# Two weight chunks of the next expert split ahead of a branch, and the work around the join put in another order

## The chip, the core and the metric

The kernel runs on one core of a Trainium2 chip. The metric is the time of one execution on the device in microseconds (us), the median of the runs shown. The engines are TensorE (PE in the rows, its weight loads PEld), VectorE (DVE), ScalarE (ACT), GpSimd (POOL) and SyncE (SP), which issues most DMAs.

## The reference

Causal attention is followed by two mixture-of-experts layers on 1792 tokens of width 768. Each layer has 8 experts with two weight matrices (768 x 1024 and 1024 x 768); each token goes to one expert, and in the first layer about half of the tokens skip.

```python
for e in range(E):                       # first layer
    mask = e_idx == e
    h = np.maximum(xc[mask] @ w1[e], 0.0)
    y[mask] = gate_w[mask, None] * (h @ w2[e])
out[do_compute] = xc + y
...
for e in range(E):                       # second layer
    mask = expert_idx == e
    h = np.maximum(x[mask] @ w1[e], 0.0)
    out[mask] = gate_w[mask, None] * (h @ w2[e])
```

## The kernel before

Attention takes the first 235 us or so and is not touched. After it the sixteen experts (`i` = 0 to 15; `m` = 0 for the first layer, `i // 8`) run one after the other. The tokens of an expert are fetched by an index list (an indirect DMA on GpSimd, `gather`) in tiles of 128.

**Split operands.** All products are made of float32r parts: a weight chunk `raw` is split into an upper part `hi` (a cast on ACT, L734) and a lower part `lo` (raw minus hi on DVE, L738, written over `raw`). `w1` has six chunks of 128x1024 (`KC`), `w2` eight of 128x768 (`FC`). The tokens are transposed on PE (L752) in two halves, and each half is split in the same way into `xt`: the upper part on ACT (L758), the lower on DVE (L759). A first product (`layer1`, L779) of one half `u` of the hidden columns takes twelve matmuls on upper weight parts (token upper and token lower, for each of six chunks) and six on lower weight parts. Then the hidden tile goes through PE transposes (`turn_h`) and is split again (`split_ht`: ACT L770, DVE L771), and `layer2` (L787) takes six matmuls for each of the eight chunks `f`.

**A tile.** `Tile.begin` holds the first product, the splits of this expert's `w2` (`w2_high`, `w2_low`; in the first tile of an expert, and not for the first expert of a layer) and `layer2` for f = 0 to 5. `Tile.finish` holds `layer2` for f = 6 and 7, the transposes and splits of the next tile's tokens, the write of the result (`put_y`), and, in the last tile of an expert, the splits of all six `w1` chunks of the next expert and the DMA issues for a later one. Six rooms `hi1` hold the upper parts. In the second layer `begin` also computes the gate in steps (`gate_parts`, small DVE operations); in the first layer it routes the tokens of the tile before into the second layer (`route_enter`, `route_turn`, `route_logits`, `route_pick`, `route_rank`, and `route_put` in `finish`).

**The branch and the join.** How many tiles an expert has is known only on the chip. Behind the first `begin` stands `tc.If(nmore[e] > 0)` (L1096): with one tile all engines go straight to the last `finish`, with more they go through the further tiles first (a nested `If` at L1077). What stands behind the point where the paths join counts on semaphores whose values both paths must reach. On the path that skips, each engine adds the missing count itself when it has done all it has to do before the branch. So an instruction behind the join that needs another engine's earlier work waits until that engine has come to the join. A wait that the rows put down to `PEq L1096` or `DVEq L1077` is of this kind.

**Order.** The schedule is written out by hand: each engine takes its instructions in the order of the code. Experts 0, 1, 2, 3, 5, 6 of the first layer and 0, 4, 7 of the second (`i` = 8, 12, 15) have one tile in this data; `i` = 4, 9 and 13 have two, `i` = 10 three, `i` = 7, 11 and 14 four.

Of the kernel before, what the change touches and what calls it, by code (L numbers as in the profile page):

```python
# [8 lines left out]
F32R = mybir.dt.float32r  # L9
# [36 lines left out]
def moe_attention_kernel(tc, qk, vv, w_r, emb, tau, w11, w12, w21, w22, out):  # L46
# [25 lines left out]
    with ExitStack() as top:  # L72
# [612 lines left out]
        with ExitStack() as ctx:  # L685
# [4 lines left out]
            def keep(shape, dt, name, pool=wp):  # L690
                return pool.tile(shape, dt, tag=name, name=name)
# [3 lines left out]
            hi2 = [keep([P, DM], F32R, f"hi2_{j}") for j in range(FC)]  # L695
            xt = keep([P, KC, P, 2], F32R, "xt")
# [24 lines left out]
            def w1(i, k):  # L721
                n = KC * i + k
                return hi1[k], lo1[n % N1], raw1[n % N1]
# [49 lines left out]
            def layer1(i, u, ks, low):  # L773

                for k in ks:
                    wh, wl, _ = w1(i, k)
                    terms = [(0, wl)] if low else [(0, wh), (1, wh)]
                    for j, r in terms:
                        nc.tensor.matmul(p1[u], xt[:, k, :, j], r[:, u * 512 : (u + 1) * 512],  # L779
                                         start=(k == 0 and j == 0 and not low), stop=(k == KC - 1 and low))  # L780
# [159 lines left out]
            class Tile:  # L940
# [22 lines left out]

                def begin(self):
# [5 lines left out]
                    self.w2_low(0)  # L970
                    layer1(i, 0, range(KC), False)
# [3 lines left out]
                    layer1(i, 0, range(KC), True)  # L975
                    self.step()
                    self.w2_low(1)
# [5 lines left out]
                    layer1(i, 1, range(KC), False)  # L983
# [19 lines left out]
                    self.w2_low(5, 6)  # L1003
# [3 lines left out]
                    self.w2_low(7)  # L1007
                    split_ht(turned, 4)
                    layer2(i, 2)
                    layer2(i, 3)  # L1010
                    if route:
                        route_rank()
                    layer2(i, 4)
                    layer2(i, 5)

                def finish(self, idx, last, nxt, route):
# [14 lines left out]
                    high(0, 1, 2)  # L1031
# [5 lines left out]
                    low(0, 1, 2)  # L1037
# [3 lines left out]
                    high(3)  # L1041
                    low(3)
                    layer2(i, 6)
                    if route:
                        route_put()
                    if nxt is not None:
                        t = xt_turn(nxt, *HALVES[1])
                        xt_split(t, *HALVES[1])
                    layer2(i, 7)
# [3 lines left out]
                    high(4, 5)  # L1053
                    put_y(self.m, self.g, idx)
                    low(4, 5)
# [140 lines left out]
```

## Time and profile before

| | |
|---|---|
| median of 3 runs | 910.62 us (909.84 to 916.43) |
| the profiled execution | 913.13 us, its span 911.3 us |
| PE busy | 832.6 us, 91% of the span |
| DVE busy | 554.6 us, 61% |
| ACT busy | 474.3 us, 52% |
| mean granted TensorE clock | 0.979 of full speed |

The profiled execution takes 1.8 us more than its span, and 2.5 us more than the median. A busy PE is one with a matmul in flight; matmuls overlap, so an idle time that the profile shows is less than what a wait costs. The experts take from about 245 us to 902 us.

### The profile page before, as it was taken

How to read it: one execution, taken by the hardware profiler on the slowest of the kernel's cores; microseconds unless marked ns; L12 is line 12 of the kernel's file. 1: busy time of each engine (PE TensorE's matmuls, PEld its weight loads, DVE VectorE, ACT ScalarE, POOL GpSimd, SP SyncE). 2: the span in 40 equal slices, each digit the busy share in tenths (PEclk: the TensorE clock that was granted, in tenths of full speed). 3: DMA queues.
4: the chain of work that ended last, by engine and by line, in shares of the span. 5: the costliest groups of instructions: out<-in, count | busy, mean ns of one | idle time of the engine just before them, and what ended most of it. 6: DMA issues, size and time to landing. Idle time of an engine off the chain costs nothing. (4 is left out here: it accounts for less than half of the span.)

```text
span 911.3 us, 14892 instructions
## 1 busy us (share of the span) xinstructions
PE 832.6 (91%) x4960; PEld 682.8 (75%) x4960; DVE 554.6 (61%) x1641; ACT 474.3 (52%) x1013; POOL 163.3 (18%) x150
## 2 busy tenths in 40 slices
PE   8998989989788888998899979899999998899995
PEld 5666666666477776886699857788889887798884
DVE  5767767776567587387743265755383368483363
ACT  5777666766456366166631153654272267372362
POOL 1132404013211333032011011111020012021000
PEclk9999999999899899999999989999999999999998
DMA  7979555564646477167610172762171076371000
GB/s 219 326 266 302 165 183 163 166 218 125 197 168 243 158 294 284 63 237 294 262 65 27 67 269 67 286 257 110 56 296 37 37 306 228 126 271 51 19 29 7
DMA packets 59033, 158.23 MB, mean 174 GB/s; under 512 B 13013, under 2 KB 23765, under 8 KB 58448
## 3 DMA queue, kind: packets, MB, share of 16 engines
q1 hardware_dynamic: 52816, 139.33, 42.8%
q0 software_dynamic: 6080, 17.29, 5.3%
q8 instruction: 59, 0.97, 0.4%
q14 instruction: 78, 0.64, 0.2%
HBM read 146.45 MB, written 22.92 MB: 186 GB/s over the span
## 5 line engine op out<-in xcount | busy, mean ns | idle before, releaser
L738 DVE TENSOR_TENSOR lo<-raw,hi 128x768 fp32r<-128x768 f32 (+1 forms) x218 | 221.7, 1064 | 37.3 <-ACT hi L734 34.4
L787 PE MATMUL p<-hi,ht 128*128 128x384 f32 x960 | 240.8, 352 | 3.4 <-DVE ht L771 2.7
L779 PE MATMUL p<-hi,xt 128*128 128x512 f32 x720 | 184.8, 401 | 25.3 <-DVE xt L759 15.8
L734 ACT CAST hi<-raw 128x768 fp32r<-128x768 f32 (+1 forms) x218 | 187.3, 924 | 35.3 <-PEq L1096 29.9
L779 PEld LDWEIGHTS p<-hi,xt 128*128 128x128 f32 x720 | 138.1, 195 | 61.1 <-DVE xt L759 22.4
L787 PEld LDWEIGHTS p<-hi,ht 128*128 128x128 f32 x960 | 166.7, 190 | 11.5 <-DVE ht L771 7.3
L321 ACT ACTIVATE pr<-st,mn 112x336 f32<-112x336 f32 x192 | 99.5, 519 | 61.6 <-DVE mn L318 61.5
L787 PE MATMUL p<-lo,ht 128*128 128x384 f32 x480 | 123.6, 339 | 0.0
L771 DVE SCALAR_TENSOR_TENSOR ht<-tp,ht 128x512 fp32r<-128x512 f32 x60 | 41.4, 689 | 126.9 <-ACT ht L770 115.1
L779 PE MATMUL p<-lo,xt 128*128 128x512 f32 x360 | 100.8, 410 | 4.9 <-DVE lo L738 4.9
L787 PEld LDWEIGHTS p<-lo,ht 128*128 128x128 f32 x480 | 88.1, 189 | 0.0
L779 PEld LDWEIGHTS p<-lo,xt 128*128 128x128 f32 x360 | 67.1, 195 | 20.7 <-DVE lo L738 11.0
L938 ACT COPY hs<-p 128x512 f32<-128x512 f32 x60 | 34.9, 582 | 91.6 <-PE p L779 88.4
L318 DVE CUSTOM_DVE_ANT_0 st<-s,mask 112x336 f32<-112x336 f32 x144 | 63.5, 465 | 30.5 <-PE s L307 18.9
L770 ACT ACTIVATE ht<-tp 128x512 fp32r<-128x512 f32 x60 | 36.0, 600 | 77.4 <-PE tp L796 74.5
L758 ACT CAST xt<-tp 128x384 fp32r<-128x384 f32 (+2 forms) x62 | 30.3, 494 | 80.9 <-PE tp L752 74.2
L759 DVE TENSOR_TENSOR xt<-tp,xt 128x384 fp32r<-128x384 f32 (+2 forms) x62 | 33.5, 542 | 57.2 <-ACT xt L758 56.9
L741 POOL DMA_INDIRECT g_r<-x,L x14 | 32.3, 2308 | 166.0 <-DVE pv L813 97.0
L331 PE MATMUL tp<-ident,pr 112*112 112x112 f32 x480 | 58.0, 269 | 0.0
L816 POOL DMA_INDIRECT out<-py,pidx x18 | 23.7, 1318 | 187.7 <-DVEq L1077 70.8
L307 PE MATMUL s<-qk 64*112 64x112 f32 (+2 forms) x288 | 50.4, 456 | 6.3 <-DVE mn L318 6.2
L331 PEld LDWEIGHTS tp<-ident,pr 112*112 112x112 f32 x480 | 47.8, 138 | 8.9 <-issue 8.1
(201 smaller groups left out, 955.0 us busy)
## 6 DMA issues: line engine op xcount, KB each, us to landing
raw<-in_w SPq DMA_DIRECT2D x96, 512.0 KB
raw<-in_w SPq DMA_DIRECT2D x128, 384.0 KB
qk<-in_qk SPq DMA_DIRECT2D x23, 896.0 KB
x<-x SPq DMA_DIRECT2D x24, 448.0 KB
v<-in_vv SPq DMA_DIRECT2D x4, 1344.0 KB
qk<-in_qk SPq DMA_DIRECT2D x2, 448.0 KB
g_n<-x,L POOLq DMA_INDIRECT x23, 6.1
out<-py,pidx POOLq DMA_INDIRECT x18, 3.4
```

What stands on the lines that cost most here:

```text
L307: nc.tensor.matmul(a[c], src[r : r + 64, c * CP : (c + 1) * CP], src[r : r + 64, S : S + n], start=True, stop=True)
L318: nc.vector.tensor_tensor_reduce(out=so, in0=a[c], in1=mask[:, S - n : S], scale=-0.125, scalar=3.0e38, op0=ALU.add, op1=ALU.min, accum_ou ...
L321: return lambda: nc.scalar.activation(a["pr"][:, OFF[c] * CP : OFF[c] * CP + n], so, AF.Exp, bias=mn, scale=-1.0, accum_out=rs)
L331: nc.tensor.transpose(tp[:, u * CP : (u + 1) * CP], pr[:, o : o + CP], ident[:CP, :CP])
L734: copy(hi, raw)
L738: eng.tensor_tensor(lo, raw, hi.bitcast(F32), op=ALU.subtract)
L759: nc.vector.tensor_tensor(xt[:, a:b, :, 1], src, hi.bitcast(F32), op=ALU.subtract)
L770: nc.scalar.activation(hi, src, AF.Relu)
L771: nc.vector.scalar_tensor_tensor(lo, src, 0.0, hi.bitcast(F32), op0=ALU.max, op1=ALU.subtract)
L779: nc.tensor.matmul(p1[u], xt[:, k, :, j], r[:, u * 512 : (u + 1) * 512], start=(k == 0 and j == 0 and not low), stop=(k == KC - 1 and low))
L787: mm = nc.tensor.matmul(p2[u], l, r[:, u * (DM // 2) : (u + 1) * (DM // 2)], start=(f == 0 and j == 0), stop=(f == FC - 1 and j == len(ter ...
L938: nc.scalar.copy(hs[:, u * 512 : (u + 1) * 512], p1[u])
```

## The change

The number of rooms for upper parts of `w1` grows from six to eight, used in turn over all chunks of all experts. The first tile of an expert splits chunks 0 and 1 of the next expert (`ahead`) behind its `layer2(3)`, before the branch. In `finish` the DMA issues stand first, then the first half of the next tokens, and only then the splits of chunks 2 to 5; `route_put` and `put_y` stand last. In `begin` the first product takes four chunks of upper parts of half 0, three of half 1, then the rest of half 0 and the lower parts; `route_enter` and `w2_low(0)` move behind that, and `w2_low(6)` and `w2_low(7)` move behind the second `split_ht`.

```diff
+            hi1 = hi1 + [keep([P, DF], F32R, f"hi1_{j}") for j in range(KC, KC + 2)]
...
-                return hi1[k], lo1[n % N1], raw1[n % N1]
+                return hi1[n % len(hi1)], lo1[n % N1], raw1[n % N1]
...
+                def ahead(self, k):
+
+                    if self.first and self.i + 1 < len(experts):
+                        split_high(self.i + 1, k)
+                        split_low(self.i + 1, k, nc.vector)
+
                 def begin(self):
...
                     self.w2_high(0, 1, 2, 3)
-                    self.w2_low(0)
-                    layer1(i, 0, range(KC), False)
+                    layer1(i, 0, range(4), False)
+                    layer1(i, 1, range(3), False)
+                    layer1(i, 0, range(4, KC), False)
+                    self.step()
+                    layer1(i, 0, range(KC), True)
                     if route:

                         route_enter()
-                    layer1(i, 0, range(KC), True)
-                    self.step()
-                    self.w2_low(1)
+                    self.w2_low(0, 1)
                     copy_h(0)
...
-                    layer1(i, 1, range(KC), False)
+                    layer1(i, 1, range(3, KC), False)
...
-                    self.w2_low(5, 6)
+                    self.w2_low(5)
                     layer2(i, 0)
                     layer2(i, 1)
                     turned = turn_h(1)
-                    self.w2_low(7)
                     split_ht(turned, 4)
+                    self.w2_low(6, 7)
                     layer2(i, 2)
                     layer2(i, 3)
                     if route:
                         route_rank()
+                    self.ahead(0)
+                    self.ahead(1)
...
-                    high(0, 1, 2)
                     if last:
                         for k in range(KC):
                             load1(KC * i + k + N1)
                         for f in range(FC - 2):
                             load2(FC * i + f + N2)
-                    low(0, 1, 2)
                     if nxt is not None:
                         t = xt_turn(nxt, *HALVES[0])
                         xt_split(t, *HALVES[0])
-                    high(3)
-                    low(3)
+                    high(2)
                     layer2(i, 6)
-                    if route:
-                        route_put()
                     if nxt is not None:
                         t = xt_turn(nxt, *HALVES[1])
                         xt_split(t, *HALVES[1])
+                    low(2)
+                    high(3)
+                    low(3)
                     layer2(i, 7)
...
                     high(4, 5)
+                    low(4, 5)
+                    if route:
+                        route_put()
                     put_y(self.m, self.g, idx)
-                    low(4, 5)
```

On DVE, behind the join from expert 3 to expert 4, this stood before (`lo1` and `hi1` are parts of `w1` chunks with their room's number, `L864` to `L178` is `route_put`, `L804` is `put_y`):

```order
L738 TENSOR_TENSOR lo1_10_79<-raw1_10_65,hi1_0_115 128x1024
L738 TENSOR_TENSOR lo1_11_80<-raw1_11_66,hi1_1_116 128x1024
L738 TENSOR_TENSOR lo1_12_81<-raw1_12_67,hi1_2_117 128x1024
L759 TENSOR_TENSOR xt_3111<-tp_2_3129,xt_3111 128x384
L738 TENSOR_TENSOR lo1_13_82<-raw1_13_68,hi1_3_118 128x1024
L864 TENSOR_TENSOR run_165<-run_165,oh2_3141 128x8
```

And now, in the same place of DVE:

```order
L761 TENSOR_TENSOR xt_3113<-tp_2_3131,xt_3113 128x384
L761 TENSOR_TENSOR xt_3113<-tp_0_3129,xt_3113 128x384
L740 TENSOR_TENSOR lo1_12_81<-raw1_12_67,hi1_2_117 128x1024
L740 TENSOR_TENSOR lo1_13_82<-raw1_13_68,hi1_3_118 128x1024
L740 TENSOR_TENSOR lo1_0_69<-raw1_0_55,hi1_4_119 128x1024
L740 TENSOR_TENSOR lo1_1_70<-raw1_1_56,hi1_5_120 128x1024
L866 TENSOR_TENSOR run_165<-run_165,oh2_3143 128x8
```

Three lower parts of weights that stood ahead of the first half of the tokens are gone from there; the tokens are first, and four lower parts follow both halves.

On DVE, at the end of expert 4's first `begin`, up to the branch, this stood before (`ht` is the second `split_ht`):

```order
L738 TENSOR_TENSOR lo2_5_104<-raw2_5_88,hi2_5_3108 128x768
L738 TENSOR_TENSOR lo2_6_105<-raw2_6_89,hi2_6_3109 128x768
L738 TENSOR_TENSOR lo2_7_106<-raw2_7_90,hi2_7_3110 128x768
L771 SCALAR_TENSOR_TENSOR ht_3117<-tp_1_3128,ht_3117 128x4x128
L1096 COMPARE_AND_BRANCH
```

And now:

```order
L740 TENSOR_TENSOR lo2_5_104<-raw2_5_88,hi2_5_3108 128x768
L773 SCALAR_TENSOR_TENSOR ht_3119<-tp_1_3130,ht_3119 128x4x128
L740 TENSOR_TENSOR lo2_6_105<-raw2_6_89,hi2_6_3109 128x768
L740 TENSOR_TENSOR lo2_7_106<-raw2_7_90,hi2_7_3110 128x768
L740 TENSOR_TENSOR lo1_2_71<-raw1_2_57,hi1_6_3111 128x1024
L740 TENSOR_TENSOR lo1_3_72<-raw1_3_58,hi1_7_3112 128x1024
L1107 COMPARE_AND_BRANCH
```

Four instructions, two of `w2` and two of the next `w1`, now stand between the second `split_ht` and the branch, where there was none.

On PE, behind the join from expert 3 to expert 4, the first product began like this (`p1_0` and `p1_1` are the halves of the hidden columns, `L876` is `route_enter`):

```order
L779 MATMUL p1_0_3123<-hi1_3_118,xt_3111 128x512 x2
L779 MATMUL p1_0_3123<-hi1_4_119,xt_3111 128x512 x2
L779 MATMUL p1_0_3123<-hi1_5_120,xt_3111 128x512 x2
L876 LDWEIGHTS roh2_3143
L876 MATMUL pm_3130<-voh2_3144,roh2_3143 128x112
L779 MATMUL p1_0_3123<-lo1_4_73,xt_3111 128x512
```

And now:

```order
L781 MATMUL p1_0_3125<-hi1_5_120,xt_3113 128x512 x2
L781 MATMUL p1_1_3126<-hi1_2_117,xt_3113 128x512 x2
L781 MATMUL p1_1_3126<-hi1_3_118,xt_3113 128x512 x2
L781 MATMUL p1_1_3126<-hi1_4_119,xt_3113 128x512 x2
L781 MATMUL p1_0_3125<-hi1_6_3111,xt_3113 128x512 x2
L781 MATMUL p1_0_3125<-hi1_7_3112,xt_3113 128x512 x2
L781 MATMUL p1_0_3125<-lo1_4_73,xt_3113 128x512
```

Six matmuls of the other half now stand before the last two chunks of upper parts, and so before all lower parts; `route_enter` follows behind the lower parts.

## Rows read from the trace of the kernel before

**Rows 1.** Waits, 262 to 528 us: total us, times, longest us.

```profile
PE p L779 <- DVE xt L759: 12.4, 12, 1.2
...
ACT hi L734 <- PEq L1096: 22.9, 6, 4.4
```

**Rows 2.** Timeline of PE, expert 3: start us, busy us, [idle before <- releaser].

```profile
318.14 0.52 PE L752 MATMUL tp<-ident,g_r 128*128 128x128 f32 x3 [0.40 <-PEq L1096]
...
321.33 0.51 PE L779 MATMUL p<-hi,xt 128*128 128x512 f32 x1 [0.22 <-ACT xt L758]
...
329.52 2.96 PE L779 MATMUL p<-hi,xt 128*128 128x512 f32 x12
332.32 0.82 PE L832 MATMUL tp<-ident,py 128*128 128x128 f32 x6
...
338.27 0.60 PE L796 MATMUL tp<-ident,hs 128*128 128x128 f32 x4
...
343.61 0.52 PE L752 MATMUL tp<-ident,g_r 128*128 128x128 f32 x3 [0.39 <-PEq L1096]
```

**Rows 3.** Timeline of DVE, end of expert 3 and join to expert 4.

```profile
337.66 2.70 DVE L738 TENSOR_TENSOR lo<-raw,hi 128x768 fp32r<-128x768 f32 x3
340.27 0.68 DVE L771 SCALAR_TENSOR_TENSOR ht<-tp,ht 128x512 fp32r<-128x512 f32 x1
344.47 3.50 DVE L738 TENSOR_TENSOR lo<-raw,hi 128x1024 fp32r<-128x1024 f32 x3 [3.52 <-ACT hi L734]
347.89 0.55 DVE L759 TENSOR_TENSOR xt<-tp,xt 128x384 fp32r<-128x384 f32 x1
...
349.49 0.16 DVE L864 TENSOR_TENSOR run<-run,oh 128x8 bf16<-128x8 bf16 x1
...
352.23 3.22 DVE L738 TENSOR_TENSOR lo<-raw,hi 128x1024 fp32r<-128x1024 f32 x3
```

**Rows 4.** Timeline of ACT, end of expert 3.

```profile
338.97 0.60 ACT L770 ACTIVATE ht<-tp 128x512 fp32r<-128x512 f32 x1 [1.11 <-PE tp L796]
```

**Rows 5.** ACT around 305 us, then windows: PE, PEld, DVE, ACT, POOL busy, PEclk, DMA share, GB/s.

```profile
304.81 0.83 ACT L734 CAST hi<-raw 128x768 fp32r<-128x768 f32 x1 [4.83 <-DMA raw<-in_w]
...
304.00:307.00 3.00, 1.53 (x12) 1.10 (x10) 0.06 (x1) 2.19 (x5) 0.00 (x0) 1.00 0.31 110
307.00:314.00 7.00, 7.00 (x27) 6.90 (x27) 5.74 (x13) 3.17 (x5) 1.02 (x1) 0.51 0.03 10
```

**Rows 6.** Timeline of ACT and PE between the layers.

```profile
533.89 1.01 ACT L833 COPY yt<-tp 128x384 f32<-128x384 f32 x2 [2.55 <-issue]
...
536.51 2.70 PE L838 MATMUL pm<-wr,yt 128*128 128x8 f32 x12 [2.17 <-DVE tok L879]
```

**Rows 7.** Timelines of expert 12: PE, then DVE, then ACT.

```profile
740.52 0.49 PE L752 MATMUL tp<-ident,g_r 128*128 128x128 f32 x3
...
758.50 0.97 PE L787 MATMUL p<-hi,ht 128*128 128x384 f32 x4 [0.39 <-DVEq L1096]
...
760.57 0.52 PE L752 MATMUL tp<-ident,g_r 128*128 128x128 f32 x3 [0.39 <-PEq L1096]
...
744.76 3.22 DVE L738 TENSOR_TENSOR lo<-raw,hi 128x1024 fp32r<-128x1024 f32 x3
...
752.28 0.69 DVE L771 SCALAR_TENSOR_TENSOR ht<-tp,ht 128x512 fp32r<-128x512 f32 x1
...
757.76 0.68 DVE L771 SCALAR_TENSOR_TENSOR ht<-tp,ht 128x512 fp32r<-128x512 f32 x1
...
756.49 0.59 ACT L770 ACTIVATE ht<-tp 128x512 fp32r<-128x512 f32 x1
```

**Rows 8.** Timelines of expert 9: PE's first turn, DVE's second `split_ht`.

```profile
566.07 0.52 PE L752 MATMUL tp<-ident,g_r 128*128 128x128 f32 x3 [0.39 <-PEq L1096]
...
585.95 0.69 DVE L771 SCALAR_TENSOR_TENSOR ht<-tp,ht 128x512 fp32r<-128x512 f32 x1
```

**Rows 9.** Accesses of the tile g_r, 287 to 345 us: issue to landing.

```profile
DMA to landing us min/median/max: 9.7/9.7/9.7
```

## Prediction

> **What bounds the kernel now.** I read the page first: PE is busy for 91% of the span, so only its waits and its slow stretches can be won. The list of waits of the first layer's experts comes next [rows 1]: PE waits twelve times for the split tokens (L779 for DVE's L759), 12.4 us in all, five one-tile joins with two waits and two other joins with one. The second row says why: ACT, at the head of the three `w1` casts, is held for 22.9 us at six joins until PE arrives there. Behind such a join ACT and DVE first split three weight chunks and only then the tokens, while PE has only `layer2` for f = 6 and 7 to do.
>
> The timeline of PE gives the size [rows 2]. Zero of my clock is PE's first token transpose behind a join (the "turn"). From the turn of expert 3 at 318.14 to the next at 343.61 is a period of 25.47 us. The first product starts at 321.33, 3.19 after the turn, and the second half of the hidden columns begins only at 329.52: 8.19 us for 18 matmuls. In the group at 329.52 twelve take 2.80 (to 332.32), 0.233 each, so that 18 would need 4.2. The difference, 4.0, is what tokens and lower weight parts cost PE behind each such join.
>
> **The change, part by part.**
>
> *One-tile joins of the first layer.* With the tokens ahead of the weights, the wait of 0.22 falls away and the product starts at 2.97. DVE's last token split ends about then (it takes 0.55, [rows 3]), I take 3.05. Four lower parts of 1024 columns follow, 1.14 each (three from 344.47 to 347.89, [rows 3]): the last is ready at 7.6. Two chunks were split before the join, so that PE has 18 upper matmuls in a row (four chunks of half 0, three of half 1, two of half 0, two matmuls each) and then six lower ones, 24 x 0.233 = 5.6, to 8.55; the lower parts come in time. `route_enter` now needs `route_put`, behind the lower parts: DVE's `route_put`, second token split (0.55) and `put_y` took 2.74, from 349.49 to 352.23; of the 2.2 without the token split I put half, 1.1, ahead of `route_enter`, so 8.7: 0.15 lost. Then comes the rest, 329.52 to 343.61 = 14.09, less the six matmuls of half 1 already done, 1.40: 12.69. The next turn is at 8.7 + 12.69 = 21.4, not 25.47: 4.07 won per join [rows 2].
>
> This holds at four joins (2 to 3, 3 to 4, 5 to 6, 6 to 7 by the experts' numbers): 16.3. At the join from expert 1 to 2 I count nothing: ACT then waits 4.83 us for a weight transfer that ends at 304.81 [rows 5], and I take that transfer to end at the same distance from the join, so that the time won is waited there. The joins from 0 to 1 and from 4 to 5 have one wait each of the twelve, half as many. Half the gain at both would be 4.1, and the wait at the two-path join is the smaller: 3.5 (2.9 to 4.2).
>
> *DVE's arrival at the join (new).* Four DVE instructions now stand between the second `split_ht` and the branch, where none stood. PE's first token transposes behind the join wait for DVE's count too. Before, PE's second turn of hidden columns (338.27) is 5.34 before the next turn [rows 2]; ACT's part starts 0.70 later, at 338.97, and takes 0.60 [rows 4]. With the turn at 21.4 the chain is: 16.06, ACT 16.76 to 17.36, DVE's `split_ht` 0.6 (0.68 busy), two lower parts of `w2` at 0.87 (three from 337.66 to 340.27, [rows 3]), two of `w1` at 1.14: 22.0, and 0.2 for the count: 22.25. That is 0.85 late. It counts at the ends of experts 3, 5 and 6; expert 2's falls into its transfer's wait, and that of 1 is not counted above either: -2.6 (0 to -4.5, if two further instructions are late).
>
> *`route_put` and the nested join.* In the ends of experts 4 and 7 (two and more tiles) `route_put` stands ahead of `put_y` and behind the second token split, where the next step waits. Its cost is bounded by zero and by the 2.74 that it takes together with `put_y` [rows 3]. I take 0.9 at each: -1.8.
>
> *Between the layers.* Expert 7's last lower parts no longer stand ahead of the addition of the tokens (L879). The logits matmul at 536.51 waited 2.17 for that; its other operand `yt` starts at 533.89 and takes 1.01, to 534.90 [rows 6]. It can start 1.6 earlier: +1.6.
>
> Sum of the first layer: 16.3 + 3.5 - 2.6 - 1.8 + 1.6 = **17.0**.
>
> *Second layer.* Here DVE, which also computes the gate, is the chain in an expert's first tile. In expert 12 [rows 7] the turn is at 740.52, the first lower part of `w2` starts at 744.76 + 2 x 1.135 = 747.03, the first `split_ht` at 752.28 (5.25 later; 11.76 after the turn), ACT's second part 4.21 after that, at 756.49, and DVE's second `split_ht` at 757.76 (17.24). This was a join from four tiles, where three chunks were split while PE ran the tile before. After the change four lower parts come behind the tokens, to 7.6; with 0.5 for `put_y`, a quarter of those 2.2, the first `w2` part starts at 8.1, the first `split_ht` at 13.35, ACT's second part at 17.56 to 18.16, the second `split_ht` at 18.2: 0.95 late. Into experts 10, 11, 12, 14 and 15: -4.75. Into 9 and 13, behind one-tile joins, the second `split_ht` came at 585.95 - 566.07 = 19.88 [rows 8], so 18.2 is +1.68 each: +3.4. At the end of expert 12, one tile, DVE arrives at 18.2 + 0.6 + 1.74 + 2.28 + 0.2 = 23.05. PE's turn stood at 760.57 - 740.52 = 20.05, 2.07 after its `layer2` group at 758.50 [rows 7] had begun; with the 0.95 it would be 21.0, so -2.05. Sum: **-3.4**.
>
> Together 17.0 - 3.4 = 13.6. The profiled execution of 913.13 becomes 899.5; it lay 2.5 above the median, so the forecast is **897.0**. A wait for code at the joins has no row that shows it apart, and the code only moves; I count zero.
>
> **The rivals.**
>
> *The transfer wait in expert 2 goes too.* ACT's issues and casts lie in another order now, and the wait of 4.83 could shrink or move. Then the fourth gain of 4.1 counts, and with it up to the 4.83 and the slow stretch behind it: from 307 to 314 the granted clock is 0.51 [rows 5], 7.00 x 0.49 = 3.4 lost. Taken together 4.1 to 12.3; at 9, **888**. Against it: the DMA share falls from high to 0.31 in that window [rows 5], so a transfer did end there. Chance 0.10. The Trainium skill ("Runtime: NRT & Kernel Launch", Instruction fetch mechanics) says that a taken branch leaves the sequential prefetch and that the engine must wait for its code; by that rule such a wait would move with the code. The rows put it down to a weight's landing and show no fetch apart.
>
> *DVE is not late.* If the two `w2` parts run beside ACT's work, or the new order gives DVE slack that I don't see, the terms of -2.6 and -2.05 fall away, and part of -4.75: **888**. For it: DVE stood idle 3.52 before its group at 344.47 [rows 3]. Chance 0.13.
>
> *The next tokens come too late.* The gather of the following tile's tokens follows the last row of `put_y`, which ended at 352.23, 8.62 after the turn at 343.61; now it is 7.6 + 2.2 and a little, 10.0. It lands 9.7 later [rows 9], at 19.7, against a turn at 21.4 to 22.25: a margin of 1.7 to 2.5. Where it lands 4 later than that (a queue that is full of weights), five joins lose 1.6 each: **905**, no change to speak of. Chance 0.18.
>
> *TensorE falls to its lower clock.* New single waits of 1.5 to 2 us stand where two short ones stood: at the ends of experts 3, 5, 6, 12, and for the second `split_ht` in up to five first tiles. Around 304 to 307 PE was busy for 1.53 of 3.00, with a granted clock of 1.00, and from 307 to 314 it was 0.51, which is 1.2 of 2.4 GHz [rows 5]. Each fall costs 3.4, nine places up to 31. Four use up the gain of 13.6, so it decides from the fifth on; six give 897 + 20.6 = **917**. Against it: at the joins of before two waits of up to 1.2 [rows 1] lay close together, and the group that followed ran at 0.233 a matmul [rows 2], which is full speed. Chance 0.09. The Trainium skill ("TensorE: Matmul & The Clock Gate", Why this matters for your kernels) warns of idle stretches of TensorE between bursts of matmuls, since the clock falls after them; it speaks against merging waits into longer ones. The row of 304 to 307 agrees, those of the joins show no fall.
>
> *The change doesn't do what it says.* The rooms or the counts could hold `ahead` back until the join, as before; then tokens first alone is left, and the lower parts come too late for PE: about **908**. Chance 0.03.
>
> **How the numbers follow.** The forecast has 0.47; DVE's arrival (0 to -4.5), `route_put` (0 to -5.5) and the second layer's five joins (0 to -9.5, if each is twice as late) spread it from 889 to 906. A measurement here can tell about 1%, 9 us, from no change: faster means below 901.5. The forecast's case lies there with 0.40, and the first two rivals with 0.23: faster 0.63. Within 1%: the rest of the forecast 0.07, late tokens 0.18, nothing done 0.03: 0.28. Slower: the clock, 0.09. The range of 886 to 908 holds all but the clock and the ends of the other cases.
>
> **What would show it.** In the changed kernel's trace the waits of L781 for the token splits in 262 to 528 should be gone but for one or two; from a one-tile turn to the next 21 to 22.5 us, not 25.5, with a wait for DVE's count at L1107 of up to 1 us; `layer2` waiting for `ht` for some 1 to 1.5 us in first tiles of the second layer; the logits matmul some 1.6 us earlier; ACT's wait of about 4.8 us in expert 2 still there. I am wrong if PE waits for the gathered tokens at its turn, if the granted clock shows new stretches at 0.5, or if the period stays above 24.

## The result and the profile after

The changed kernel takes 902.41 us (median of 4 runs, 900.77 to 904.86) against 911.18 for the kernel before (median of 4); the ratio is 0.988, with a 95% interval of 0.984 to 0.992. The forecast was 897.0 in a range of 886 to 908. The profiled span is 901.1 (911.3 before).

From the first part of the page of the changed kernel (busy us, share of the span, instructions), and two groups of its fifth part (busy, mean ns | idle before, releaser):

```profile
PE 824.0 (91%) x4960; PEld 686.5 (76%) x4960; DVE 554.4 (62%) x1641; ACT 474.8 (53%) x1013; POOL 135.2 (15%) x150
...
L781 PE MATMUL p<-hi,xt 128*128 128x512 f32 x720 | 183.3, 403 | 8.0 <-PEq L1088 3.3
L736 ACT CAST hi<-raw 128x768 fp32r<-128x768 f32 (+1 forms) x218 | 187.3, 923 | 0.6 <-DMA raw<-in_w 0.6
```

ACT's 22.9 us of waiting for PE ahead of the `w1` casts [rows 1] are gone, and so is PE's wait for the token splits. What PE waits for now, from 245 to 528 us (us in total, times, longest):

```profile
PE tp L754 <- DVEq L1107: 7.1, 5, 2.7
PE pm L840 <- ACT yt L835: 3.2, 1, 3.2
PE p L781 <- DVEq L1088: 2.5, 2, 1.5
PE tp L798 <- ACT hs L940: 2.4, 1, 2.4
```

PE's timeline for expert 3, which answers to [rows 2]:

```profile
316.83 0.52 PE L754 MATMUL tp<-ident,g_r 128*128 128x128 f32 x3 [0.69 <-DVEq L1107]
...
319.63 4.35 PE L781 MATMUL p<-hi,xt 128*128 128x512 f32 x18
323.81 1.55 PE L781 MATMUL p<-lo,xt 128*128 128x512 f32 x6
...
339.17 0.52 PE L754 MATMUL tp<-ident,g_r 128*128 128x128 f32 x3 [1.24 <-DVEq L1107]
```

Eighteen upper matmuls stand in one group without a wait, 2.80 after the turn, and six lower ones behind them. The period is 339.17 - 316.83 = 22.34 (25.47 before; 22.25 forecast with DVE's late arrival). DVE's end of that expert, which answers to [rows 3]:

```profile
334.32 0.69 DVE L773 SCALAR_TENSOR_TENSOR ht<-tp,ht 128x512 fp32r<-128x512 f32 x1 [0.17 <-ACT ht L772]
334.93 4.09 DVE L740 TENSOR_TENSOR lo<-raw,hi 128x768 fp32r<-128x768 f32 x4
```

The four lower parts end at 339.02, and PE's turn follows 0.15 later: this is the 1.24 wait.

The whole account is read from the times between the turns (PE's first token transposes of a tile to those of the next; differences of starts in PE's timelines). The two columns on the right are runs of the next section.

| tile | before | after | rooms_only | ahead_only |
|---|---|---|---|---|
| expert 1 | 24.89 | 26.23 | 24.94 | 25.91 |
| expert 2 | 30.44 | 29.57 | 31.11 | 29.63 |
| expert 3 | 25.46 | 22.34 | 23.18 | 22.02 |
| expert 4, first tile | 24.90 | 20.98 | 22.62 | 20.63 |
| expert 4, second | 23.16 | 25.92 | 23.16 | 24.04 |
| expert 5 | 22.82 | 22.33 | 22.82 | 21.99 |
| expert 6 | 25.40 | 22.33 | 23.14 | 22.01 |
| expert 7, first | 24.90 | 20.96 | 22.62 | 20.61 |
| expert 7, last, and between the layers | 41.75 | 41.75 | 41.79 | 41.72 |
| expert 9, first (13 alike) | 22.14 | 20.45 | 19.86 | 19.23 |
| expert 11, first (10, 14 alike) | 19.51 | 20.41 | 19.50 | 18.84 |
| expert 12 | 20.05 | 22.96 | 20.03 | 21.39 |
| expert 8's turn to the end of the span | 363.6 | 366.5 | 358.4 | 354.2 |

The spans differ by 10.2; 1.8 of it lies ahead of expert 0's turn (244.75 and 242.96), in code that is the same. So the experts of the first layer won 11.4 and those of the second lost 2.9. In the traces of all runs below that first stretch takes 242.3 to 249.1 us, though no edit lies in it. Medians that differ by a few us are therefore weak evidence, and the periods are read first.

### The profile page after: what moved, and what is told of

It reads as the page before. It is cut to its first block, busy times and chain, and to the rows that moved or that the text cites. A ratio compares the mean times of both kernels' runs of the same rounds, so it can differ in the third digit from the quotient of the medians.

```text
span 901.1 us, 14898 instructions
## 1 busy us (share of the span) xinstructions
PE 824.0 (91%) x4960; PEld 686.5 (76%) x4960; DVE 554.4 (62%) x1641; ACT 474.8 (53%) x1013; POOL 135.2 (15%) x150
## 5 line engine op out<-in xcount | busy, mean ns | idle before, releaser
L781 PEld LDWEIGHTS p<-hi,xt 128*128 128x128 f32 x720 | 140.4, 198 | 37.4 <-ACTq L1088 5.1
L781 PE MATMUL p<-lo,xt 128*128 128x512 f32 x360 | 96.2, 402 | 0.0
L781 PEld LDWEIGHTS p<-lo,xt 128*128 128x128 f32 x360 | 67.8, 195 | 11.4
L818 POOL DMA_INDIRECT out<-py,pidx x18 | 19.7, 1093 | 207.7 <-ACT hi L736 75.5
L342 PE MATMUL av<-pt,v 112*64 112x448 f32 (+3 forms) x384 | 50.6, 405 | 0.0
```

What stands on the lines that cost most here:

```text
L342: nc.tensor.matmul(av[u * D : (u + 1) * D, j * CP :], v_t[b][:, j, 2 * hp + u, :], pts[2 * g + u][:, o : o + (NCH - j) * CP], start=(j == ...
```

## The experiments

Each ran beside the kernel before, whose median lay between 911.18 and 914.85 on the four occasions; the ratio is to that one, so ratios are compared and not medians. "Ahead" in a name is the split of chunks 0 and 1 written ahead of the branch.

| run | median us | ratio (95%) |
|---|---|---|
| the change | 902.41 | 0.988 (0.984 to 0.992) |
| ahead_only | 887.9 | 0.973 (0.969 to 0.976) |
| w2_order_back | 900.2 | 0.986 (0.982 to 0.989) |
| second_layer_old | 894.44 | 0.979 (0.975 to 0.983) |
| paced_loads | 904.52 | 0.991 (0.988 to 0.994) |
| rooms_only | 902.77 | 0.988 (0.985 to 0.992) |
| tokens_first_only | 954.92 | 1.044 (1.041 to 1.047) |
| ahead_old_product | 901.19 | 0.987 (0.985 to 0.989) |
| ahead_old_puts | 890.09 | 0.973 (0.970 to 0.976) |
| rooms_7 | 904.37 | 0.989 (0.984 to 0.995) |
| ahead_alone | 898.56 | 0.983 (0.979 to 0.987) |
| ahead_nested_paced12 | 881.37 | 0.963 (0.959 to 0.968) |
| rooms_nested_paced12 | 876.88 | 0.960 (0.956 to 0.965) |

### Which part gains: four runs on the changed kernel

**ahead_only** puts the splits behind the join back in front of the tokens:

```diff
+                    high(2)
                     if last:
...
+                    low(2)
                     if nxt is not None:
                         t = xt_turn(nxt, *HALVES[0])
                         xt_split(t, *HALVES[0])
-                    high(2)
+                    high(3)
+                    low(3)
                     layer2(i, 6)
...
-                    low(2)
-                    high(3)
-                    low(3)
```

> Splits ahead of the branch, rooms and the first product's order as in the changed kernel; behind the join the old order with chunk 2 and its lower part ahead of the tokens. Theory (the chunks split ahead carry the gain, since PE gets 18 upper matmuls without a wait): one chunk ahead of the tokens costs at most the 1.0 of a cast and the 1.1 of a lower part, of which PE's layer2(6) and (7) hide most; the turn-to-turn time of expert 3 rises from 22.3 to at most 23.5 and the time is 901 to 906. Rival (tokens first carries the gain): the period of expert 3 goes back to 24.5 or more, PE waits twice per join for the token splits again, and the time is 907 to 911.

It came out at 887.9, far better than both forecasts. The period of expert 3 fell to 22.02 instead of rising, and a first tile of the second layer takes 18.84, where the change needs 20.41. Putting the tokens first is therefore not what gains: it costs the change about 14 us. In expert 11 of the changed kernel DVE stands idle for the tokens and all lower parts come late:

```profile
652.94 0.56 DVE L761 TENSOR_TENSOR xt<-tp,xt 128x384 fp32r<-128x384 f32 x1 [3.75 <-ACT xt L760]
654.32 0.56 DVE L761 TENSOR_TENSOR xt<-tp,xt 128x384 fp32r<-128x384 f32 x1 [0.82 <-ACT xt L760]
654.79 4.62 DVE L740 TENSOR_TENSOR lo<-raw,hi 128x1024 fp32r<-128x1024 f32 x4
...
665.17 0.69 DVE L773 SCALAR_TENSOR_TENSOR ht<-tp,ht 128x512 fp32r<-128x512 f32 x1
```

The same stretch of ahead_only, on DVE, has one lower part done before PE's turn and one between the two halves of the tokens (turn 644.18, against 651.84 above), so that the first `split_ht` is 11.75 after the turn instead of 13.33:

```profile
641.83 1.23 DVE L740 TENSOR_TENSOR lo<-raw,hi 128x1024 fp32r<-128x1024 f32 x1 [0.29 <-ACT hi L736]
645.28 0.56 DVE L761 TENSOR_TENSOR xt<-tp,xt 128x384 fp32r<-128x384 f32 x1 [2.23 <-ACT xt L760]
646.22 1.23 DVE L740 TENSOR_TENSOR lo<-raw,hi 128x1024 fp32r<-128x1024 f32 x1 [0.38 <-ACT hi L736]
...
655.93 0.68 DVE L773 SCALAR_TENSOR_TENSOR ht<-tp,ht 128x512 fp32r<-128x512 f32 x1
```

**w2_order_back** puts two lower parts of `w2` back ahead of the second `split_ht`:

```diff
-                    self.w2_low(5)
+                    self.w2_low(5, 6)
...
+                    self.w2_low(7)
                     split_ht(turned, 4)
-                    self.w2_low(6, 7)
```

> The lower parts 6 and 7 of w2 go back ahead of the second split_ht. Theory (PE's new wait for DVE's count at the join is the row of four DVE instructions behind split_ht): two of 0.87 leave it, 1.7, so the waits of 1.24 at the ends of experts 3, 5 and 6 vanish and that of 2.4 at the end of expert 12 falls below 0.8; the periods of 3, 5 and 6 fall from 22.3 to about 21.1. In first tiles of the second layer the two parts now stand ahead of DVE's second split_ht, which costs up to 1.7 at seven places where DVE is the chain. Together 898 to 905. Rival (PE waits for something else that DVE does late, the token gather's row or the splits ahead themselves): the waits of 1.24 stay above 0.8 and the time is 902 or more.

The time is in the range, the mechanism only half. PE's waits for DVE's count (L1107) fell from 9.5 to 4.5 us, that at the end of expert 3 from 1.24 to 0.70. But PE's waits for `ht` rose, here of this run from 262 to 910 us (in the changed kernel 4.6 in four waits, and 3.8 in three that are put down to the gate step behind `ht`):

```profile
PE p L789 <- DVE ht L773: 12.1, 15, 1.3
PE tp L754 <- DVEq L1107: 4.5, 5, 1.8
```

DVE has no idle time there for the two parts (the changed kernel shows 0.17 ahead of `split_ht`); they delay `split_ht` or the branch. The period of expert 3 is 22.09, not 21.1, and expert 11's first tile 21.06 instead of 20.41. Who waits changes; the sum hardly does.

**second_layer_old** keeps the new order in the first layer and takes the orders of before from the end of expert 7 on; only the eight rooms stay there, and the new first product in expert 8's first tile. Of its diff, which repeats the old lines under this condition, the splits:

```diff
-                    if self.first and self.i + 1 < len(experts):
+                    if self.first and self.i + 1 < NE:
...
+                    if i + 1 >= NE:
+                        high(0, 1, 2)
                     if last:
...
+                    if i + 1 >= NE:
+                        low(0, 1, 2)
```

> From the end of expert 7 on every order is the old one, first layer as in the changed kernel. From the first turn of expert 8 to the end of the span it was 363.5 before and 366.5 after. Theory (the new order costs the second layer 3 us because DVE is the chain of its first tiles, and four lower parts behind the tokens delay it): this stretch goes back to 363 to 364 and the time to about 899.5. Rival (the 3 us are the clock's and chance): the stretch stays at 365 to 367, the time at 902.

From expert 8's turn to the end it took 897.3 - 539.2 = 358.1, less than either kernel, so both sides were wrong. Expert 13's first tile takes 19.92 where the kernel before needed 22.19, though its code behind that join has the order of before. ACT's timeline at that join, with PE's turn at 750.21:

```profile
746.90 2.00 ACT L736 CAST hi<-raw 128x1024 fp32r<-128x1024 f32 x2 [0.17 <-ACTq L1133]
750.00 1.05 ACT L736 CAST hi<-raw 128x1024 fp32r<-128x1024 f32 x1 [1.10 <-issue]
```

Two casts that stand behind the join in the code run 3 us before PE comes to it, and the third waits. With six rooms in fixed places a cast overwrites what the expert's own first product has read, and that count on PE is one that both paths must reach; with eight rooms in turn the first two casts overwrite rooms of an older expert. A new theory follows: the rooms lift the wait by themselves.

**tokens_first_only** has the eight rooms and the new order without `ahead`, so that all six chunks are split behind the tokens:

```diff
                 def ahead(self, k):
-                    if self.first and self.i + 1 < len(experts):
+                    if False:
...
-                    high(2)
+                    high(0, 1, 2)
...
-                    low(2)
+                    low(0, 1, 2)
```

> The changed kernel with eight rooms and its new order, but without the splits ahead of the branch: all six chunks of w1 are split behind the join, behind the first half of the tokens. Theory (tokens first costs, because ACT and DVE stand idle until the tokens are turned and all lower parts follow them): the last lower part is ready at about 9.9 instead of 7.6 after the turn, PE waits for it and for the last casts, first tiles of the second layer are later by 2 or more, and the time is 907 to 916. Rival (tokens first is a gain by itself): 900 to 905.

The direction is the theory's, the size far above its range: 4.4% slower than before. PE's waits from 262 to 960 us:

```profile
PE p L781 <- DVE lo L740: 23.3, 41, 0.6
PE p L789 <- DVE ht L773: 9.5, 7, 2.0
PE p L781 <- ACT hi L736: 8.3, 14, 0.6
```

First tiles of the second layer take 24.55. A part of the size is TensorE's clock: its mean is 0.953 here and 0.979 before, which is an estimated 25 us of its span of 958. Spare rooms don't help where the cast stands in ACT's queue behind a token split that waits for PE.

### The rooms by themselves

**rooms_only** and **rooms_7** are the kernel before with one edit (two spare rooms, or one: `KC + 1`):

```diff
+            hi1 = hi1 + [keep([P, DF], F32R, f"hi1_{j}") for j in range(KC, KC + 2)]
...
-                return hi1[k], lo1[n % N1], raw1[n % N1]
+                return hi1[n % len(hi1)], lo1[n % N1], raw1[n % N1]
```

> The kernel before with eight rooms for upper parts in turn instead of six, and no other edit. Theory (formed from the run with the second layer's old order, where ACT casts two chunks 3 us before PE comes to a one-tile join although the code has them behind it: the casts waited at the join because PE's count released their rooms, and two spare rooms lift that wait alone): ACT's wait of 22.9 us for PE at six joins falls below 12, PE's twelve waits for token splits nearly vanish, the first layer's one-tile periods fall from 25.5 to 22 to 23, and the time is 886 to 896. Rival (the new order of the code is needed for it, above all the splits written ahead of the branch): periods stay above 24.5 and the time is 905 or more.

> The kernel before with seven rooms in turn, one spare instead of two. Theory (each spare room lets one cast and one lower part pass a one-tile join before PE): half the gain of eight rooms; the period of expert 3 is 24 to 24.6 (25.5 with six rooms, 23.2 with eight) and the time 906 to 910. Rival (the two rooms gain because all twelve waits need both chunks out of the way): the period stays above 25 and the time within 2 of before.

The mechanism is the theory's in both. ACT's wait for PE in front of the casts, 262 to 528 us, is 22.9 with six rooms [rows 1], 15.3 with seven and 1.5 with eight; the period of expert 3 is 25.46, 24.33 and 23.18, that of expert 9's first tile 22.14, 20.99 and 19.86: 1.1 for each room. With eight, the join into expert 4 reads on ACT (PE's turn is at 344.46):

```profile
340.60 2.00 ACT L735 CAST hi<-raw 128x1024 fp32r<-128x1024 f32 x2 [0.18 <-ACTq L1097]
344.24 1.05 ACT L735 CAST hi<-raw 128x1024 fp32r<-128x1024 f32 x1 [1.64 <-issue]
```

The times fit less well. Two rooms alone give 902.77, above the range of 886 to 896: PE still waits for the second token split (0.67 in expert 3) and a lower part (0.63), the stall of expert 2 treated below is long (31.11), and the stretch ahead of expert 0's turn takes 2.4 more than before. One room gives 904.37, below its range of 906 to 910; its expert 2 took 26.99, again the stall. The point that counts is that **two rooms alone are worth what the whole change is worth**, 0.988 both. Counted from expert 0's turn to the end, the traces even give them 13.5 us and the change 8.4.

**ahead_alone** adds to rooms_only the splits ahead of the branch and nothing else:

```diff
                     layer2(i, 3)
...
+                    self.ahead(0)
+                    self.ahead(1)
...
-                    high(0, 1, 2)
+                    high(2)
...
-                    low(0, 1, 2)
+                    low(2)
```

> The kernel before with eight rooms and with the splits of chunks 0 and 1 written ahead of the branch, every other order as before. Theory (at one-tile joins the rooms have already done this; written ahead it helps only behind experts of two or more tiles, whose next first tile in the second layer falls from 19.5 to about 18.9, and costs nothing at the join, since only two DVE instructions follow split_ht): one-tile periods within 0.4 of those with rooms alone (23.2 for expert 3), time 896 to 901. Rival (writing it ahead carries the gain down to 888): 892 or less.

898.56, as the theory had it: expert 3 takes 23.12 (23.18 with rooms alone). But expert 11's first tile stayed at 19.48; the 0.6 that the theory gave to the early split do not come from it. In ahead_old_product, below, that tile takes 18.86 with the old first product, and in w2_order_back undoing the move of `w2_low(6)` and `(7)` alone cost 0.65: so it is mainly that move that shortens these tiles.

### The rest of the new order

**ahead_old_product** takes ahead_only and puts the first product, `route_enter` and `w2_low(0)` back:

```diff
-                    layer1(i, 0, range(4), False)
-                    layer1(i, 1, range(3), False)
-                    layer1(i, 0, range(4, KC), False)
-                    self.step()
-                    layer1(i, 0, range(KC), True)
+                    self.w2_low(0)
+                    layer1(i, 0, range(KC), False)
                     if route:
                         route_enter()
-                    self.w2_low(0, 1)
+                    layer1(i, 0, range(KC), True)
+                    self.step()
+                    self.w2_low(1)
```

> The run with the splits ahead and the old order behind the join (887.9), with the first product, route_enter and the first lower parts of w2 in their old order too. Theory (with two chunks ahead, upper parts are ready when PE wants them, and lower parts come 1.1 apart while PE takes one in 0.23, so the interleaved first product saves at most 0.5 at a join): 886 to 891. Rival (the 18 upper matmuls in a row carry the gain): the one-tile periods rise by 1 or more, 895 or more.

The rival's number came (901.19; 23.57 for expert 3), not its reason. PE waits here not for weights but for `route_put`, which now stands behind the lower parts while `route_enter` is early again. PE, expert 3:

```profile
318.05 2.95 PE L781 MATMUL p<-hi,xt 128*128 128x512 f32 x12
322.40 0.21 PE L878 MATMUL pm<-voh,roh 128*128 128x112 f16 x1 [1.40 <-DVE voh L178]
```

In the second layer, which routes nothing, first tiles are as in ahead_only (18.86 and 18.84). So the interleaved product is worth nothing there; in the first layer it covers the later `route_put`. **ahead_old_puts** takes ahead_only and puts `route_put` and `put_y` back ahead of the last lower parts:

```diff
                     layer2(i, 6)
+                    if route:
+                        route_put()
...
+                    put_y(self.m, self.g, idx)
                     high(4, 5)
                     low(4, 5)
-                    if route:
-                        route_put()
-                    put_y(self.m, self.g, idx)
```

> The same run with route_put and put_y in their old places ahead of the last lower parts. Theory (route_put behind the second token split holds up the nested joins of experts 4 and 7, about 1 us each, and the slow clock at 366 stands behind the first of them): the second tile of expert 4 takes 23 to 23.3 instead of 24.0, and the time is 884 to 888, unless the last two lower parts, 2.2 later on DVE, hold up PE at one-tile joins. Rival (they do): PE waits for lower parts by 0.5 or more at each, 889 to 894.

890.09, in the rival's range, but no wait of PE for a lower part of `w1` shows. Expert 4's second tile falls from 24.04 to 23.18, as forecast, and the one-tile periods of experts 3, 5 and 6 rise by 0.6 (22.61, 22.55, 22.74). Against ahead_only the intervals overlap.

### The stalls of experts 1 and 2

In the changed kernel ACT's next instruction comes late in both, with nothing that the profile names as its releaser. Expert 2, on ACT, and the windows (PE, PEld, DVE, ACT, POOL busy, PEclk, DMA share, GB/s):

```profile
299.29 0.48 ACT L835 COPY yt<-tp 128x384 f32<-128x384 f32 x1 [0.52 <-ACT hi L736]
304.63 0.48 ACT L835 COPY yt<-tp 128x384 f32<-128x384 f32 x1 [4.86 <-issue]
```

```profile
299.00:302.00 3.00, 2.94 (x21) 2.62 (x19) 2.52 (x3) 0.48 (x1) 1.41 (x1) 1.00 1.01 388
302.00:305.00 3.00, 0.00 (x0) 0.00 (x0) 0.00 (x0) 0.37 (x1) 0.00 (x0) 1.00 0.17 58
```

PE, DVE and ACT all stand, ACT between two like copies of one loop, and it goes on when the DMA share has fallen from 1.01. **paced_loads** spreads the burst:

```diff
-                        for f in range(FC - 2):
-                            load2(FC * i + f + N2)
...
+                def layer2_load(self, f, *more):
+                    name = layer2(self.i, f)
+                    if self.first and self.i:
+                        for c in (f, *more):
+                            load2(FC * (self.i - 1) + c + N2, after=name)
```

> The eight w2 loads of each expert no longer follow the six w1 loads at the join; each waits for one layer2 step of the next expert's first tile. Theory (in experts 1 and 2 ACT stands 5.9 and 4.9 us with nothing to wait for in the profile because its next code is fetched behind the burst of weights, which fills all 16 DMA engines for some 16 us): with the burst halved both stalls fall below 2 us, PE's waits of 2.4, 2.7 and 3.2 there shrink, the slow clock at 288 goes, and the time is 892 to 898. Rival (the stalls are no fetch, or the fetch is slow by itself): both stalls stay within 1 us of their length and the time is 901 to 904; where the later loads come too late for w2, ACT waits for raw and the time is above 904.

The stalls fell from 5.91 to 3.28 and from 4.86 to 2.26 (the view puts these two shorter ones down to a matmul and to a lower part of a weight, which the two copies don't read), and experts 1 and 2 took 25.24 and 25.25 (26.23 and 29.57). The time did not follow: 0.991 against 0.988, with intervals that overlap. In the trace the second tile of expert 13 takes 25.11 instead of 19.52; PE waits there, and then runs at half the clock (18 matmuls in 7.18), while the DMA engines are busy. That the later loads are in the way there is a reading of one trace. PE of this run, with its window:

```profile
781.04 7.18 PE L781 MATMUL p<-hi,xt 128*128 128x512 f32 x18 [3.80 <-PEq L1089]
```

```profile
777.00:780.00 3.00, 0.24 (x2) 0.00 (x0) 1.79 (x8) 1.52 (x3) 0.85 (x1) 1.00 0.87 314
```

So each theory had half: about 2.6 of each stall goes with the burst, and 3.3 and 2.3 stay. The Trainium skill ("Runtime: NRT & Kernel Launch", Instruction fetch mechanics) says that an engine fetches its code by a DMA queue of its own, and that behind a taken branch it must wait for that where the target isn't fetched yet. The traces agree with it, though no row says for which engine a fetch is. Transfers of 8 KB stand on the queue q14, whose kind the profile calls instruction. In 13 of the 14 traces (all but tokens_first_only) one of them lands 0.9 to 1.5 us before ACT goes on, at both stalls. In paced_loads it is all that the DMA engines move from 277 to 279 us, and ACT goes on at 280.18 (`--dma` over that window):

```profile
DMA packets 1, 0.01 MB, mean 4 GB/s; under 512 B 0, under 2 KB 0, under 8 KB 0
q14 instruction: 1, 0.01, 1.0%
```

So what stays without the burst most likely waits for code too. Why that fetch takes so long, no run shows.

### Two combinations

**ahead_nested_paced12** is ahead_only with two edits: `route_put` early where the tile isn't an expert's last, and the paced loads in experts 1 and 2 alone (`self.i in (1, 2)`). **rooms_nested_paced12** is the same with `ahead` empty and `high(0, 1, 2)`, `low(0, 1, 2)` first behind the join.

```diff
                     layer2(i, 6)
+                    if route and not last:
+                        route_put()
...
-                    if route:
+                    if route and last:
                         route_put()
```

> The run with the splits ahead and the old order behind the join (887.9), with two edits: route_put in its old, early place in tiles that are not an expert's last, and the w2 loads paced by the layer2 steps in experts 1 and 2 only. Theory: the nested join of expert 4 wins 0.9 (its second tile 24.0 to 23.2), and the code-fetch stalls of experts 1 and 2 go, as where all loads were paced: 25.9 to 25.2 and 29.6 to 25.3. Nothing is lost in experts 5, 6, 9 and 13, where pacing had put the burst in the way of other code. 880 to 884. Rival (the stalls move on into the next code that is fetched): 886 or more.

> The same as the run with early route_put and paced loads, but the splits of chunks 0 and 1 stand first behind the join again, so that on the chip only the spare rooms let them pass it. Theory (written ahead of the branch they make PE wait 1.2 for ACT's or DVE's count at each one-tile join, which falls to 0.4 here; behind experts of more tiles they come later, 0.6 in each of five first tiles of the second layer): periods of 3, 5 and 6 near 21.2 instead of 22.0, first tiles of the second layer near 19.4, and 879 to 885, within 3 of that run. Rival (the order in the code matters more than the wait at the join): 888 or more.

The first came out as its theory had it, 881.37; expert 2 took 25.61, expert 4's second tile 23.17. The second, 876.88, lies below its range of 879 to 885, though the two intervals overlap: its experts 1 and 2 took 22.08 and 23.91 instead of 25.16 and 25.61, which no forecast had. Without `ahead` in the code PE no longer waits for DVE's count at the join; PE of the last run, expert 3, period 21.17:

```profile
308.58 0.52 PE L754 MATMUL tp<-ident,g_r 128*128 128x128 f32 x3 [0.39 <-DVE lo L740]
...
311.38 4.34 PE L781 MATMUL p<-hi,xt 128*128 128x512 f32 x18
...
329.75 0.52 PE L754 MATMUL tp<-ident,g_r 128*128 128x128 f32 x3 [0.40 <-DVE lo L740]
```

The first tiles of experts 10, 11 and 14 took 18.84, not 19.4, with `ahead` and without: the early split behind longer experts, which that forecast had priced at 0.6, is worth nothing. This version is 4% faster than the kernel before and beats the change too (0.960, interval to 0.965, against 0.984 and more).

## Why the prediction was right, and where its steps failed

The time lies in the range, 5.4 above the forecast. It misses the prediction's own limit for faster, 901.5, to which 0.63 was given, by 0.9. Of the 10.2 us between the two spans the experts gave 8.4, where 13.6 was forecast; the 1.8 ahead of them come from code that is the same, and are luck. Two of its own signs of being wrong showed up in part: new stretches at half the clock, and one wait for gathered tokens.

**One-tile joins, with DVE's arrival: right.** 4.07 less 0.85 was forecast for experts 3 and 6, and 3.12 and 3.07 were won; 4.07 for the first tiles of 4 and 7, and 3.92 and 3.94 were won. The chain for DVE (22.25, though its terms add up to 22.2) met 22.34, and the 0.2 for the count, which no row gave, came as 0.15. The chain for expert 12 (23.05) met 22.96, the first `split_ht` of the second layer (13.35) met 13.33.

**The second layer: right where it was worked out, and lucky in the sum.** -3.4 was forecast, -2.9 came: 0.9 lost at joins from longer experts (expert 11; 1.3 and 1.5 in experts 10 and 15), 1.7 won in expert 9, 2.9 lost at expert 12. The second tile of expert 13 won 1.8 that no term had; PE's wait of 1.79 there without a releaser is gone.

**The joins from 0 to 1 and from 4 to 5: wrong.** They were given 3.5. Expert 5 won 0.5; expert 1 lost 1.3. The wait of 3.2 that ACT had in expert 1 before, which the prediction passed over, grew to 5.9, PE waited 2.4 for it and then 2.7 at the branch, and ran at half the clock behind that.

**Expert 2: close, for another reason.** Nothing was counted, and 0.9 was won. The wait of 4.83 that the prediction took for a weight's transfer [rows 5] is still there with 4.86, but between two copies that need no weight: it is the stall treated above.

**Between the layers: mostly given back.** The logits no longer wait for the addition of the tokens, and PE is 2.5 earlier there (5.23 from the first filler matmul behind `layer2`, L129, to the logits before, 2.77 now). But the gather of the next tokens now waits for the write of the last rows. GpSimd before (1.05 is the gather, released by DVE) and after:

```profile
543.91 1.05 POOL L741 DMA_INDIRECT g_r<-x,first  x1 [2.97 <-DVE first L197]
```

```profile
524.00 0.99 POOL L856 DMA_INDIRECT x<-py,pidx  x1 [12.23 <-DVE eq L848]
530.12 1.45 POOL L743 DMA_INDIRECT g_r<-x,first  x1 [5.13 <-DMA x<-py,pidx]
```

PE waits 2.77 for these tokens, and from the logits to the next turn it takes 12.86 instead of 11.26. Of 2.46 won, 0.86 is left, where +1.6 was forecast. The period of 41.75 doesn't show it, since the nested join of expert 7 lies in it and lost as much.

**The nested joins: right, but for the clock.** 0.9 was given at each. In expert 7 PE's waits at the join went from 1.10 to 1.96, 0.86 more; in expert 4 from 1.24 to 2.02, 0.78 more. PE before (expert 4) and after (experts 4, 4 and 7):

```profile
372.67 3.21 PE L779 MATMUL p<-hi,xt 128*128 128x512 f32 x12 [1.24 <-PEq L1077]
```

```profile
364.13 0.48 PE L781 MATMUL p<-hi,xt 128*128 128x512 f32 x1 [1.06 <-PEq L1088]
365.58 5.79 PE L781 MATMUL p<-hi,xt 128*128 128x512 f32 x17 [0.96 <-DVEq L1088]
...
498.25 4.24 PE L781 MATMUL p<-hi,xt 128*128 128x512 f32 x17 [1.52 <-DVEq L1088]
```

In expert 4 PE then runs at half the clock for 3.4 us, another 1.7. Windows of the changed kernel in experts 2, 4 and 13:

```profile
288.40:291.80 3.40, 3.40 (x13) 3.27 (x12) 2.04 (x3) 2.90 (x4) 0.00 (x0) 0.50 0.98 360
366.90:370.30 3.40, 3.40 (x10) 2.63 (x9) 0.00 (x0) 0.00 (x0) 0.00 (x0) 0.50 0.02 2
752.60:756.00 3.40, 3.40 (x13) 3.21 (x11) 2.25 (x4) 3.12 (x5) 0.00 (x0) 0.50 0.86 289
```

This is the rival of the clock, at three new places instead of five or more, and each costs 1.7, half of the 3.4 that the prediction took from a fall of twice the length. The falls came behind waits of 2.74 (at 287.26) and 2.40 (at 751.18) and the pair of 1.06 and 0.96; none came right behind the single waits of 1.24 or the 2.38 at 279.43 in expert 1. The slow stretch in expert 2 behind ACT's stall [rows 5] stayed.

**What carries it: the step that failed unseen.** The prediction credited the code's order: tokens ahead of the weights, two chunks split ahead, 18 upper matmuls in a row. The runs show that two spare rooms alone give the change's whole gain (0.988), and that the tokens' place costs about what the rest of the order adds. DVE's late arrival needs `ahead` in front of the branch together with what else was moved there: PE's wait at the end of expert 3 is 0.40 without `ahead` (rooms_nested_paced12), and 0.40 too with `ahead` in the old order (ahead_alone). The row that could have told is the second of [rows 1]: the casts waited for PE at the join, and for them the question was what on PE they needed, which was a room. The number was right with the sum of the effects; the parts were not told apart.

## What to carry to other kernels

Where an engine waits at a branch for another one, ask first which buffer the other holds: one more buffer let the work pass the join here without a line moved and without a wait at the branch, while work written ahead of it must be finished before anyone goes on. An engine that is idle while another turns its input should get work that needs nothing from it, so weights that are ready go ahead of tokens that are not. A burst of loads issued in one place can also be in the way of transfers that no row names as a releaser, here most likely code; spreading it shortened two stalls, and in one trace another stood elsewhere.

## What was not expected of the hardware

Issuing eight loads of 384 KB some 12 to 18 us later behind the turn took 2.6 us off two stalls of ACT. In the changed kernel these have no releaser in the profile, and in 13 of 14 traces they end 0.9 to 1.5 us behind an 8 KB transfer on the instruction queue; in one trace PE waited 3.8 us elsewhere at a DMA share of 0.87. PE's clock fell to half at three new places, for 3.4 us each, behind single waits of 2.74 and 2.40 and a pair of 1.06 and 0.96, and not right behind a single one of 2.38.
